# Sliding-window attention for two problems on one core: where the first V weights are issued, how many output staging buffers there are, and who casts and stores the last output tile

## The chip, the cores and the metric

The kernel runs on one core of a Trainium2 chip. The metric is the device time of one execution in microseconds (us), lower is better. All tensors in memory are bf16; the matrix products accumulate in f32.

## The reference, cut to what matters

Two independent problems, A and B, have the same shapes: `x` is 2048 rows of 1024, `wqkv` is 1024 x 3072 and `wo` is 1024 x 1024. Each is one attention layer with 32 heads of 32 columns and a causal window of 256 keys; the two results stand side by side in the output.

```python
qkv = (x @ wqkv).reshape(B, S, 3, H, Dh)              # S=2048, H=32, Dh=32
q, k, v = ...                                          # per head
scores = einsum("bhqd,bhkd->bhqk", q, k) * (Dh ** -0.5)
mask = (i - j >= 0) & (i - j < 256)
p = softmax(where(mask, scores, -1e9))
o = einsum("bhqk,bhkd->bhqd", p, v)
return o.reshape(B, S, D) @ wo
# result: concatenate([A, B], axis=-1), 2048 x 2048
```

## The kernel before, in words

The work is laid out for TensorE (PE), which is to be kept busy from start to end. `x` is held transposed, in tiles `xT` of 512 rows (four per problem, k = 0 to 3). Heads are taken in groups of four (128 columns); there are 8 groups per problem, 16 in all. A group needs its Q and K projections (`wqk` weights, lines 197 to 213) and its V projection (`wv` weights, two groups at a time, lines 215 to 236). Attention then runs in sessions of four key-by-query blocks: scores into PSUM (`st`, line 427), one exponential on ACT (line 435), two masks on POOL (lines 443 and 447), then products with V and with ones into `acc` (line 488), a reciprocal and a multiplication on DVE (lines 498 and 503) into `oT`.

The projections and the output products are cut into chains of eight matmuls. A planner with its own clock and cost table (`emit`, `level`, `forced`, `start_chain`) spreads these chains over the sessions. Each chain owns one of two PSUM banks (`pp`, pool `ps_proj`), and its result is moved out by `evacuate`, which picks ACT (line 189) or DVE (line 191) by the planner's clock. The order on each engine is the order in which the program is written; nothing reorders it afterwards.

**The start.** Rows of problem A's first 512 are loaded as they are (`xrow`, four transfers of 128 rows, in the buffer of an `oT` tile) on the SP queue, and PE transposes them (`flip`, line 549; ACT copies half of each result at line 553, DVE the other half at line 554, from the same PSUM bank). The other three tiles of A are transposed by DMA (`load_x`, line 132). The first weights, `wqk` for group 0 (two transfers of 256 KB) and `wv` for groups 0 and 1 (512 KB), are issued on ACT's queue, lines 520 to 522. A one-column POOL copy (line 524) reads `xrow[2]` and writes into the first `xT` tile that the DMA transposes: the transposing transfer, which writes the same tile, therefore waits on SP until the third set of rows has landed. Behind it on SP stand the two `wqk` transfers for group 1, the transposes of tiles 2 and 3 and the second `wv`.

**Loads later on.** Weights and B's `x` are loaded in pieces. `load_piece` writes one column with POOL (line 327) between two masks, and the piece's DMA on SP waits for that. SP is one queue in order: an output store that stands behind such a piece is issued after it.

**The output.** `out_steps` (lines 238 to 255) makes one 128 x 512 block of the output: eight matmuls, a cast into a staging tile `osb`, and a store on SP (line 252). `osb` comes from the pool `misc`, which has two buffers for each of its names. A cast into a buffer waits until the store that last read the buffer has landed. The casts of 21 of the 64 blocks start after 576 us, behind the last attention block. The last block is the last work of the kernel; after it each engine passes the branch at line 778, which skips a slower path for large inputs.

Of the kernel before, what the change touches and what calls it, by code (L numbers as in the profile page):

```python
# [8 lines left out]
BF16 = mybir.dt.bfloat16  # L9
# [9 lines left out]
P = 128  # L19
# [59 lines left out]
def _fast_path(ctx, tc, cfg, problems, outs, consts, certify):  # L79
    nc = tc.nc  # L80
    S, D, CT, T, NB = cfg.S, cfg.D, cfg.CT, cfg.T, cfg.NB
# [30 lines left out]
    ptp = ctx.enter_context(tc.tile_pool(name="pt", bufs=7))  # L112
    edgep = ctx.enter_context(tc.tile_pool(name="edge", bufs=2))
    misc = ctx.enter_context(tc.tile_pool(name="misc", bufs=2))
    once = ctx.enter_context(tc.tile_pool(name="once", bufs=1))
    ps_st = ctx.enter_context(tc.tile_pool(name="ps_st", bufs=1, space=PSUM))
    ps_acc = ctx.enter_context(tc.tile_pool(name="ps_acc", bufs=2, space=PSUM))
# [2 lines left out]
    xT, wqk, wv, wo_sb, vts, oTs, qks, pts = {}, {}, {}, {}, {}, {}, {}, {}  # L120
# [6 lines left out]
    def new_x(pi, k):  # L127
        xT[(pi, k)] = xpool.tile([P, CT, 512], BF16, name="xT")
# [7 lines left out]
    def wsrc(pi):  # L136
        return problems[pi][1].rearrange("(ct p) (k n) -> p ct k n", p=P, k=3)
# [4 lines left out]
    def load_wqk(g, which, queue, lo=0, hi=CT):  # L142
        pi, t = divmod(g, T)
        queue.dma_start(out=wqk[g][:, lo:hi, which, :],
                        in_=wsrc(pi)[:, lo:hi, which, t * P:(t + 1) * P])
# [4 lines left out]
    def load_wv(m, lo, hi, queue):  # L150
        pi, mm = divmod(m, T // VG)
        w_ = VG * P
        queue.dma_start(out=wv[m][:, lo:hi, :],
                        in_=wsrc(pi)[:, lo:hi, 2, mm * w_:(mm + 1) * w_])
# [14 lines left out]
    def by_columns(out, lo, hi, lhsT, rhs, start, stop):  # L169
        if whole[0]:  # L170
            nc.tensor.matmul(out[:, lo:hi], lhsT=lhsT, rhs=rhs, start=start, stop=stop,  # L171
                             skip_group_check=True)
            return
        for c in range(0, P, 32):
            nc.tensor.matmul(out[c:c + 32, lo:hi], lhsT=lhsT[:, c:c + 32], rhs=rhs, start=start,  # L175
                             stop=stop, tile_position=(0, c), skip_group_check=True)
# [10 lines left out]
    def evacuate(out, in_, engines=("act", "dve")):  # L187
        if clock.evacuate(engines) == "act":
            nc.scalar.copy(out=out, in_=in_)  # L189
        else:  # L190
            nc.vector.tensor_copy(out=out, in_=in_)

    def new_pp():
        clock.chain()
        return ps_proj.tile([P, 512], F32, name="pp")
# [42 lines left out]
    def out_steps(pi, b, ch):  # L238
        k, a = divmod(b, QB)
        st_ = {}  # L240
        steps = []
        for ct in range(CT):
            def f(ct=ct):
                if ct == 0:
                    st_["pp"] = new_pp()
                by_columns(st_["pp"], 0, 512, oTs[(pi, k)][:, ct, a * P:(a + 1) * P],
                           wo_sb[(pi, ch)][:, ct, :], ct == 0, ct == CT - 1)
                clock.pe += NS_MM
                if ct == CT - 1:
                    osb = misc.tile([P, 512], BF16, name="osb")  # L250
                    evacuate(osb[:], st_["pp"][:])
                    nc.sync.dma_start(out=outs[pi][b * P:(b + 1) * P, ch * 512:(ch + 1) * 512],
                                      in_=osb[:])
            steps.append((NS_MM, f))
        return steps

# [73 lines left out]
    chains = []  # L330
# [36 lines left out]
    current = []  # L367
# [149 lines left out]
    xrow = [rows[:, 2 * a:2 * a + 2, :].rearrange("p t n -> p (t n)") for a in range(QB)]  # L517
    for a in range(QB):
        nc.sync.dma_start(out=xrow[a], in_=problems[0][0][a * P:(a + 1) * P, :])
    for which in range(2):  # L520
        load_wqk(0, which, nc.scalar)
    load_wv(0, 0, CT, nc.scalar)
    new_x(0, 1)
    nc.gpsimd.tensor_copy(out=xT[(0, 1)][:, 0, 0:1], in_=xrow[2][:, 0:1])
    load_x(0, 1)
# [199 lines left out]
def kernel(  # L725
# [46 lines left out]
    with tc.manual_schedule():  # L772
        with ExitStack() as fctx:
            _fast_path(fctx, tc, cfg, problems, outs, consts, [reduce_bits, decide])
# [40 lines left out]
```

## Time and profile before

| | |
|---|---|
| median of 4 runs | 617.95 us (616.85 to 618.6) |
| the profiled execution | 618.5 us, span 616.7 us |
| PE busy | 594.5 us, 96% of the span |
| DVE busy | 505.5 us, 82% |
| ACT busy | 440.5 us, 71% |
| POOL busy | 320.2 us, 52% |
| mean granted TensorE clock | 0.995 of full |
| output stores (128 KB each, SP) | 64, median 1.7 us from issue to landing |

The span is what the profiler saw from the first to the last instruction of the core; 1.8 us of the execution's own time lie outside it. Busy times of PE are of overlapping, pipelined instructions. Lines of a timeline give the start, the duration, the engine, the source line, the operation and in brackets the idle time before it with what ended it. Lines of the chain of waits give start, duration and what the end of the kernel hung on at that time. Names ending in q (SPq, ACTq) are the queues of the engines' sequencers: a DMA's time there is that of its issue, not of its transfer.

### The profile page before, as it was taken

The numbers are of one execution on the slowest core, as the hardware profiler recorded it, in microseconds if no ns is written. First come the engines' busy times: TensorE is split into PE (matmuls) and PEld (weight loads), VectorE is DVE, ScalarE is ACT, GpSimd is POOL, SyncE is SP. The second block draws the span as 40 slices with busy tenths as digits, with TensorE's granted clock in tenths as the row PEclk, the third lists the DMA queues.
The fourth block names the chain that finished last, engine by engine and source line by source line (L and its number), as shares of the span: only waits on it lengthen the run. The fifth ranks groups of instructions, "written<-read, shape, count | busy, mean of one in ns | idle before, by whom it ended". The sixth has DMA issues, their size and how long they took to land.

```text
span 616.7 us, 27555 instructions
## 1 busy us (share of the span) xinstructions
PE 594.5 (96%) x12366; PEld 343.5 (56%) x12416; DVE 505.5 (82%) x816; ACT 440.5 (71%) x372; POOL 320.2 (52%) x631
## 2 busy tenths in 40 slices
PE   7999999999999999798999999999999999999996
PEld 5565466657555756454555665745445664444442
DVE  1588989999998999977999999887998999899200
ACT  3777878788878888666777777777877777775332
POOL 0565665655566566545555555555566555553000
PEclk9999999999999999989999999999999999999998
DMA  9923110111015501433001010112011030113222
GB/s 236 174 79 99 37 37 3 37 37 39 3 37 97 113 3 30 79 86 96 29 19 46 12 38 2 38 36 80 11 54 38 3 106 28 54 55 112 71 69 72
DMA packets 86652, 35.40 MB, mean 57 GB/s; under 512 B 65536, under 2 KB 86016, under 8 KB 86528
## 3 DMA queue, kind: packets, MB, share of 16 engines
q1 hardware_dynamic: 83408, 32.52, 21.3%
q8 instruction: 99, 1.62, 1.1%
q10 hardware_dynamic: 3120, 1.05, 0.7%
q14 instruction: 25, 0.20, 0.1%
HBM read 17.83 MB, written 8.39 MB: 43 GB/s over the span
## 4 chain that ended last, share of the span: by engine, by line
PE 86%; DMA 4%; DVE 2%; ACT 2%; issue 2%; POOL 1%; SPq 1%; ACTq 0%; DVEq 0%; POOLq 0%
PE pp L175 40%; PE pp L171 25%; PE acc L488 13%; PE st L427 9%; DMA out_dram<-osb 2%; DMA xT<-in_A_x_dram 1%; ACT pt L435 1%; DMA oT<-in_A_x_dram 1%; SPq L132 1%; DVE rinv L498 1%; POOL pt L443 1%; POOL pt L447 1%; DVE both L457 1%; ACT osb L189 0%; DVE top L183 0%
## 5 line engine op out<-in xcount | busy, mean ns | idle before, releaser
L435 ACT ACTIVATE pt<-st 128x2048 bf16<-128x2048 f32 x180 | 338.1, 1878 | 78.6 <-PE st L427 64.6
L498 DVE RECIPROCAL rinv<-acc 128x128 f32<-128x128 f32 x256 | 227.0, 924 | 31.2 <-PE acc L488 30.9
L447 POOL TENSOR_SCALAR_AFFINE_SELECT pt<-pt 128x512 bf16<-128x512 bf16 x224 | 150.8, 673 | 153.9 <-ACT pt L435 153.9
L443 POOL TENSOR_SCALAR_AFFINE_SELECT pt<-pt 128x512 bf16<-128x512 bf16 x256 | 176.4, 691 | 86.4 <-ACT pt L435 84.4
L175 PE MATMUL pp<-xT,wqk 128*32 128x512 bf16 x2688 | 160.7, 379 | 0.5 <-DMA xT<-in_B_x_dram 0.5
L457 DVE TENSOR_TENSOR both<-pt 128x512 bf16<-128x512 bf16 x224 | 130.3, 621 | 0.0
L175 PEld LDWEIGHTS <-wqk 128*32 128x32 bf16 x2688 | 71.4, 97 | 55.6 <-DMA xT<-in_B_x_dram 0.9
L171 PE MATMUL pp<-xT,wqk 128*128 128x512 bf16 (+1 forms) x331 | 80.2, 377 | 9.6 <-issue 3.3
L175 PE MATMUL pp<-wv,xT 128*32 128x256 bf16 x2548 | 78.6, 273 | 0.0
L427 PE MATMUL st<-qT,kT 32*128 32x384 bf16 (+2 forms) x1488 | 71.6, 269 | 0.8 <-ACT pt L435 0.7
L175 PEld LDWEIGHTS <-xT 128*32 128x32 bf16 x2548 | 68.3, 97 | 4.5
L171 PE MATMUL pp<-wo_sb,oT 128*128 128x512 bf16 x269 | 61.5, 379 | 2.4 <-issue 1.1
L488 PE MATMUL acc<-pt,vt 128*32 128x128 bf16 (+1 forms) x2160 | 63.4, 239 | 0.1
L189 ACT CAST osb<-pp 128x512 bf16<-128x512 f32 x52 | 30.3, 585 | 45.5 <-PE pp L171 23.1
L427 PEld LDWEIGHTS <-kT 32*128 32x128 bf16 x1488 | 22.5, 92 | 66.8 <-issue 66.3
L171 PEld LDWEIGHTS <-wqk 128*128 128x128 bf16 x368 | 34.1, 99 | 43.7 <-issue 13.8
L503 DVE TENSOR_TENSOR oT<-acc,rinv 128x256 bf16<-128x256 f32 x128 | 54.1, 423 | 3.7
L175 PE MATMUL pp<-wo_sb,oT 128*32 128x512 bf16 x920 | 54.0, 379 | 0.0
L488 PEld LDWEIGHTS <-vt 128*32 128x32 bf16 x2160 | 35.9, 96 | 26.5 <-issue 24.4
L171 PE MATMUL pp<-wv,xT 128*128 128x256 bf16 x387 | 47.3, 273 | 0.2 <-ACT kT L189 0.2
L171 PEld LDWEIGHTS <-oT 128*128 128x128 bf16 x282 | 26.8, 98 | 34.0 <-issue 3.2
L171 PEld LDWEIGHTS <-xT 128*128 128x128 bf16 x387 | 36.3, 98 | 10.4 <-issue 4.6
(43 smaller groups left out, 352.1 us busy)
## 6 DMA issues: line engine op xcount, KB each, us to landing
out_dram<-osb SPq DMA_DIRECT2D x64, 128.0 KB, 1.7
wqk<-in_B_wqkv_dram SPq DMA_DIRECT2D x32, 128.0 KB, 2.9
wqk<-in_A_wqkv_dram SPq DMA_DIRECT2D x24, 128.0 KB, 2.8
wo_sb<-in_A_wo_dram SPq DMA_DIRECT2D x16, 128.0 KB, 2.2
wv<-in_B_wqkv_dram SPq DMA_DIRECT2D x16, 128.0 KB, 2.4
wo_sb<-in_B_wo_dram SPq DMA_DIRECT2D x16, 128.0 KB, 2.3
oT<-in_A_x_dram SPq DMA_DIRECT2D x4, 256.0 KB, 5.2
wv<-in_A_wqkv_dram SPq DMA_DIRECT2D x8, 128.0 KB, 2.4
```

Source lines behind the costliest of these rows:

```text
L132: nc.sync.dma_start_transpose(out=xT[(pi, k)][:, c0:c1, lo:hi], in_=problems[pi][0][k * 512 + lo:k * 512 + hi, c0 * P:c1 * P])
L171: nc.tensor.matmul(out[:, lo:hi], lhsT=lhsT, rhs=rhs, start=start, stop=stop, skip_group_check=True)
L175: nc.tensor.matmul(out[c:c + 32, lo:hi], lhsT=lhsT[:, c:c + 32], rhs=rhs, start=start, stop=stop, tile_position=(0, c), skip_group_check=True)
L189: nc.scalar.copy(out=out, in_=in_)
L427: nc.tensor.matmul(st[:, r, a:b, :], lhsT=kT[32 * r:32 * r + 32, j * P:(j + 1) * P], rhs=qT[32 * r:32 * r + 32, q * P:(q + b - a) * P], st ...
L435: nc.scalar.activation(out=pt[:, :, :n, :].rearrange("p r a q -> p r (a q)"), in_=st[:, :, :n, :].rearrange("p r a q -> p r (a q)"), func= ...
L443: nc.gpsimd.affine_select(out=blk, in_=blk, pattern=[[0, 4], [1, P]], compare_op=ALU.is_ge, fill=0.0, base=0, channel_multiplier=-1)
L447: nc.gpsimd.affine_select(out=blk, in_=blk, pattern=[[0, 4], [-1, P]], compare_op=ALU.is_gt, fill=0.0, base=0, channel_multiplier=1)
L457: nc.vector.tensor_tensor(out=both[:, :, h, :], in0=pts[s0][:, :, a0, :], in1=pts[s1][:, :, a1, :], op=ALU.add)
L488: nc.tensor.matmul(acc[32 * r:32 * r + 32, which, o:o + w_], lhsT=lhsT, rhs=src[:, r, :, :], start=(x == 0), stop=(x == len(moves) - 1), t ...
L498: nc.vector.reciprocal(out=rinv[:, a * P:(a + 1) * P], in_=acc[:, 1, a * P:(a + 1) * P])
L503: nc.vector.tensor_tensor(out=oTs[(pi, k)][:, t, h * 256:(h + 1) * 256], in0=acc[:, 0, :], in1=rinv[:], op=ALU.mult)
```

## The change

Three edits. First, the 512 KB transfer of the first `wv` moves from ACT's queue to SP's, behind a second one-column POOL copy that reads `xrow[2]`; it now stands on SP between the row loads and the first DMA transpose. Second, `osb` gets a pool of its own with four buffers. Third, for the very last output block, ACT casts columns 0 to 287 and DVE columns 288 to 511, and the two parts are stored by ACT's queue and SP's queue; all other blocks go as before.

```diff
     misc = ctx.enter_context(tc.tile_pool(name="misc", bufs=2))
+    osbp = ctx.enter_context(tc.tile_pool(name="osb", bufs=4))
...
                 if ct == CT - 1:
-                    osb = misc.tile([P, 512], BF16, name="osb")
-                    evacuate(osb[:], st_["pp"][:])
-                    nc.sync.dma_start(out=outs[pi][b * P:(b + 1) * P, ch * 512:(ch + 1) * 512],
-                                      in_=osb[:])
+                    osb = osbp.tile([P, 512], BF16, name="osb")
+                    dst = outs[pi][b * P:(b + 1) * P, ch * 512:(ch + 1) * 512]
+                    if chains or current:
+                        evacuate(osb[:], st_["pp"][:])
+                        nc.sync.dma_start(out=dst, in_=osb[:])
+                    else:
+                        nc.scalar.copy(out=osb[:, 0:288], in_=st_["pp"][:, 0:288])
+                        nc.vector.tensor_copy(out=osb[:, 288:512], in_=st_["pp"][:, 288:512])
+                        nc.scalar.dma_start(out=dst[:, 0:288], in_=osb[:, 0:288])
+                        nc.sync.dma_start(out=dst[:, 288:512], in_=osb[:, 288:512])
...
     for which in range(2):
         load_wqk(0, which, nc.scalar)
-    load_wv(0, 0, CT, nc.scalar)
+    nc.gpsimd.tensor_copy(out=wv[0][:, 0, 0:1], in_=xrow[2][:, 0:1])
+    load_wv(0, 0, CT, nc.sync)
     new_x(0, 1)
     nc.gpsimd.tensor_copy(out=xT[(0, 1)][:, 0, 0:1], in_=xrow[2][:, 0:1])
     load_x(0, 1)
```

In the instructions as built, PE's are the same in kind and order. ACT loses one DMA issue at the start and has its last cast shorter with a DMA issue behind it; DVE gets one more cast at the end, POOL one more copy at the start, SP one more DMA at the start and a narrower one at the end. `evacuate` picks the same engine for every other block.

## The prediction

> **What bounds the kernel now.** I read the busy table first, then what PE waited for over the whole run, then the chain of waits around each of PE's gaps.
>
> ```profile
> PE 594.5 (96%) x12366; PEld 343.5 (56%) x12416; DVE 505.5 (82%) x816; ACT 440.5 (71%) x372; POOL 320.2 (52%) x631
> ```
>
> PE is busy for 594.5 of 616.7 us: only its 22 us of gaps can be won without less work. The waits of PE say whose they are (engine, line, what it waited for: us in total, times, longest).
>
> ```profile
> PE pp L171 <- ACT osb L189: 2.0, 3, 1.1
> PE pp L171 <- DMA xT<-in_A_x_dram: 0.8, 1, 0.8
> PE st L427 <- ACT pt L435: 0.7, 1, 0.7
> PE st L549 <- DMA oT<-in_A_x_dram: 0.5, 1, 0.5
> ```
>
> Three waits on an `osb` cast make 2.0 us. The largest wait, 3.2 us on POOL's `wv` pieces at 257.8 to 261.0, lies before the first `osb` and is not touched. Now the start, in the chain of waits:
>
> ```profile
> 1.73 5.73 DMA oT<-in_A_x_dram
> ...
> 7.51 0.20 POOL xT L524
> ...
> 7.72 4.06 SPq L132
> ...
> 11.84 0.57 SPq L144
> ...
> 12.45 0.58 SPq L144
> ...
> 13.07 8.90 DMA xT<-in_A_x_dram
> ...
> 22.01 2.10 PE pp L171 x9
> ```
>
> PE's first 22 us end on a chain without PE in it: the third rows land at 7.46, POOL's copy releases SP, SP issues the transpose of tile 1, two `wqk`, then the transpose of tile 2, which lands at 21.97. PE, idle for the last 0.78 us, goes on at 22.01. Whatever is won earlier by PE is lost again here.
>
> **Edit 1: wv to SP.** It takes a 2.00 us issue off ACT (1.93 to 3.93). That hides nothing of worth: ACT's table load then runs from about 1.95 to 3.2, but its first copy (5.25) needs PE's transposes, which end at 5.14. The edit adds a POOL copy (0.19 us) before the issue, and the second POOL copy runs while SP issues, so it costs nothing. On SP the issue of 512 KB lies ahead of the transpose of tile 1, both `wqk`, tiles 2 and 3 and the second `wv`. The same transfer on SP took 0.58 us to issue at 23.76; on ACT's filled queue 2.00. I take 0.6 with the gap.
>
> Its transfer moves too. DMA engines show a share of 0.95 or more from 2 us to 13 us, so 512 KB at the 277 to 330 GB/s of 7 to 9 us is 1.6 to 1.9 us of their time, now between release and first transpose. Tile 1 landed at 7.72 + 6.1 = 13.8 and is first read at 16.6: later by up to 1.9 it still is in time. `wv` itself was there at 10.1 (1.93 + 8.2). Issued at 7.7 with the 4.4 us of the second `wv` on SP it lands at 12.1; PE wants it at 12.7. Tile 3 landed at 25.8 (19.2 + 6.6) and `wqk` of group 1 is read only from 37.7; first read of tile 3 is at 28.3. Only tile 2 has no slack.
>
> How far tile 2 moves is bounded from both sides. Upper: the full 1.9 us. Lower: there is a hole in its transfer.
>
> ```profile
> 16.00:17.00 1.00, 1.00 (x10) 0.80 (x9) 0.06 (x1) 1.00 (x1) 0.00 (x0) 1.00 2.00 55
> 17.00:18.00 1.00, 0.95 (x11) 0.29 (x11) 0.64 (x1) 0.19 (x2) 0.81 (x2) 1.00 0.54 118
> ```
>
> The last column, GB/s, falls from 288 at 14 us to 55 and 118, while one 16 KB packet of the instruction queue is fetched in 15 to 18. Work that comes later may wait out the hole as tile 2 does now, so part or all of the shift vanishes. Also the rows may land sooner: at 2 to 4 us DMA moved 186 and 259 GB/s while ACT issued `wv`; at the 315 of 6 us those 445 KB take 1.4 instead of 2.0 us. More I don't grant, because the first 1.5 MB in line were rows and `wqk` and had passed only at about 7.2 us. So tile 2 moves by -0.6 to +1.9 us; I take +0.4, nearest to the 0.6 of SP's order less a part in the hole. PE's wait of 0.78 grows to about 1.2.
>
> **Edit 2: four buffers.** Each wait of PE in turn. At 283:
>
> ```profile
> 279.29 3.45 DMA out_dram<-osb
> ...
> 282.84 0.59 ACT osb L189
> ...
> 283.47 0.59 PE pp L171 x2
> ```
>
> The store before last, queued on SP behind pieces of `xT`, lands at 282.74; the cast waits for its buffer, PE 1.05 us for the bank. With a free buffer ACT casts at 280.0, when its exponential (278.14, 1.88 us) ends. PE goes on at 282.4. Next late is the scores' exponential: ready at 281.9, done at 283.8, wanted at 284.7 instead of 285.7. The 1.05 us stay won; PE shows no gap over 0.2 from there to 561. Waits of DVE (1.96 at 426.2) and ACT (1.10 at 463.1) on stores cost PE nothing. At 559 to 563:
>
> ```profile
> 558.81 0.58 ACT L189 CAST osb<-pp 128x512 bf16<-128x512 f32 x1 [2.10 <-DMA out_dram<-osb]
> ...
> 561.22 0.40 PE L427 MATMUL st<-qT,kT 32*128 32x128 bf16 x12 [0.72 <-ACT pt L435]
> ...
> 562.76 0.58 ACT L189 CAST osb<-pp 128x512 bf16<-128x512 f32 x1 [1.59 <-DMA out_dram<-osb]
> ...
> 563.40 1.89 PE L171 MATMUL pp<-wo_sb,oT 128*128 128x512 bf16 x8 [0.59 <-ACT osb L189]
> ```
>
> The late cast holds the exponential behind it on ACT, PE's scores 0.72; the next cast 0.59: 1.31 together. Next late is DVE, nearly without a gap from 555 to 572. PE's products at 569.45 need the bank that DVE's multiplication frees at 568.31 (567.90 + 0.41): 1.14 of the 1.31 are free, and DVE itself loses its 0.24 wait on a store. I take 1.2 (1.1 to 1.3). Last, 0.36 at 600.2 to 600.6, where a store took 4.1 instead of 1.7 us. Four buffers at one block per 1.73 us cover 4.1. Sum 1.05 + 1.2 + 0.36 = 2.6 us won (low 2.0, if the odd store is not there and half of 563 is lost; high 2.7).
>
> **Edit 3: the last block.** Two engines on one bank:
>
> ```profile
> 5.25 0.58 ACT L553 COPY xT<-acc 128x512 bf16<-128x512 bf16 x1
> ...
> 5.87 0.42 DVE L554 COPY xT<-acc 128x512 bf16<-128x512 bf16 x1 [4.61 <-ACT xT L553]
> ```
>
> Here too each engine took a half of one bank, and DVE began after ACT had ended. In the built order DVE's half again waits for ACT. So the casts add. ACT's 288 columns lie between 0.33 (288/512 of 0.585) and 0.585; with the slope from 512 columns (0.585) to 2048 (1.88), 0.40. DVE's 224 lie between 0.30 and 0.69; I take 0.40. In sequence 0.84 with the gap, against 0.585: SP's store is issued 0.25 later and is half as large. The last store took 2.8 us to land, the median one 1.7, so the luck of this one store swings up to 1.1 either way; ACT gets an issue of 0.3 to 0.6 ahead of its branch. I take +0.2 (-0.5 to +1.0).
>
> The Trainium skill speaks against this edit. "PSUM — Partial Sum Buffer", section "PSUM bank collisions raise a hardware error", has it that two engines must not read one bank and quadrant of partitions at once. By that rule the cost is the serial one above; by the wording of the change, two casts side by side, the last store would leave about 0.2 sooner. "DMA: Bandwidth & Descriptors", "Issuing engines are not separate DMA queues", adds that a second issuing engine saves issue time only.
>
> **Sum.** -2.6 + 0.4 + 0.2 = -2.0 us. The profiled execution (618.5, of which 616.7 span) becomes 616.5; it is 0.55 above the median of 617.95, which becomes 616.0. From no change a measurement of this kernel tells about 0.2%, 1.24 us.
>
> **The rivals.** (a) Slower: the weights block the queue. If `wv` on SP takes the 8.2 us of its ACT row, it lands at 15.9; PE waits 3.2 at 12.7, and tile 2 behind it lands 5.8 later (15.9 less 10.1). Then -2.6 + 5.8 + 0.2 = +3.4: 621.3. It beats the gain once tile 2 lands 2.4 us later than now. For it: SP is in order and the DMA engines are full. Against: those 8.2 us held 1 MB of rows and `wqk` ahead, which have nearly passed by 7.7; the second `wv` took 4.4. (b) No change: the whole 1.9 us reach tile 2, the tail costs 0.5: -2.6 + 1.9 + 0.5 = -0.2, 617.8. For it: the full DMA engines. Against: the hole. (c) The staging buffers don't do what they promise, because DVE and ACT take over as bound around 560: only 283 and a little more is won, -1.3 + 0.4 + 0.2 = -0.7, 617.3. Against: DVE's slack of 1.14. (d) Holding back does work: rows 0.6 sooner, shift swallowed, tail as lucky as the median store: -2.6 - 0.6 - 0.5 = -3.7, 614.3.
>
> **How the numbers follow.** The forecast gets 0.52; (a) 0.10, (b) 0.18, (c) 0.08, (d) 0.12. The main case spans 615.2 to 616.7 (-1.3 to -2.8). The range runs from 614.5, into (d), to 617.9, past (b), and leaves (a) out. Faster by over 0.2% (below 616.7) is the main case and (d): 0.64. (b) and (c) are the same: 0.26. Slower: (a), 0.10.
>
> **What would show it.** Right: PE's waits on `osb` at 283, 563 and 600 and the 0.72 on `pt` are gone, DVE's last cast begins after ACT's, PE's wait on `xT` at 22 us is about 1.2 instead of 0.78, and SP shows a `wv` issue at 7.7 of about 0.6 us. Wrong: a PE wait on `wv` near 12.8, a new PE wait on DVE near 568, tile 2 landing before 21.9 or after 24, or a tail from the last matmul to the end that differs from the present 5.6 us (611.1 to 616.7) by more than 1.

## The result, and the profile after

The changed kernel takes 616.52 us in the median (612.98 to 621.32), the kernel before 618.34 (615.35 to 623.82) in the runs beside it. The ratio is 0.9974, with a 95% interval of [0.9963, 0.9984]: 1.6 us less, between 1.0 and 2.3. The forecast was 2.0 less. The profiled execution took 614.69 us with a span of 613.0, so the two profiles lie 3.8 us apart, over twice what the medians say. That difference needs an explanation of its own.

The busy table shows the same work as before, in a shorter span:

```profile
PE 593.7 (97%) x12366; PEld 343.6 (56%) x12416; DVE 507.8 (83%) x817; ACT 440.6 (72%) x372; POOL 321.2 (52%) x632
```

The waits of PE (engine, line, what it waited for: us in total, times, longest). Lines have moved by one to eight: 171 is 172 now, 189 is 190, 427 is 434, 435 is 442, 549 is 557.

```profile
PE pp L172 <- POOL wv L334: 3.1, 1, 3.1
PE acc L557 <- DMA oT<-in_A_x_dram: 1.4, 2, 0.9
...
PE pp L172 <- DMA xT<-in_A_x_dram: 1.1, 1, 1.1
PE st L557 <- DMA oT<-in_A_x_dram: 0.6, 1, 0.6
PE pp L172 <- POOL xT L334: 0.3, 1, 0.3
```

No line names `osb` any more, and the 0.7 on `pt` is gone. The 0.5 on a piece of B's `xT` (line 175 before) is gone too, which no edit aimed at. The wait on A's `xT` is 1.1 instead of 0.8. The waits on the rows (`oT`) are not shorter: 1.4 and 0.6, where they were 1.3 and 0.5.

The start, in the chain of waits (start, duration, what the end hung on):

```profile
1.73 5.94 DMA oT<-in_A_x_dram
...
7.72 0.19 POOL wv L529
7.91 0.13 POOL xT L532
8.04 0.28 SPq L154
...
8.37 5.00 SPq L133
...
13.42 0.57 SPq L145
...
14.04 0.58 SPq L145
...
14.66 9.17 DMA xT<-in_A_x_dram
...
23.88 2.10 PE pp L172 x9
```

The third rows land at 7.67, not sooner than the 7.46 of before. Between them and the first transpose stand now two POOL copies and the issue of `wv` (8.04), and the issue of tile 1 itself takes 5.00 us where it took 4.06. Tile 2 lands at 23.83 instead of 21.97, which is 1.86 later. PE's wait on it grew by only 0.3, because PE itself came 1.56 later to the place; why is told under the hardware.

The hole in the transfers moved along with the work. The windows of a microsecond have the busy times of PE, PEld, DVE, ACT and POOL, then the granted clock, the DMA share and GB/s:

```profile
16.00:17.00 1.00, 1.00 (x16) 0.53 (x15) 0.00 (x0) 0.68 (x2) 0.00 (x0) 1.00 1.23 277
...
18.00:19.00 1.00, 0.95 (x7) 0.47 (x5) 0.49 (x1) 0.69 (x1) 0.24 (x1) 1.00 0.41 6
```

Before, 55 GB/s stood at 16 us; now 6 GB/s stand at 18. The 16 KB packet of the instruction queue, beside which the prediction saw the hole, starts at 17.7 instead of 15.6. The hole did not absorb the shift.

The places where PE waited for `osb`, in the timeline (start, duration, engine, line, operation, in brackets the idle time before and its releaser):

```profile
279.30 1.00 SPq L255 DMA_DIRECT2D out_dram<-osb  x2
...
280.21 0.58 ACT L190 CAST osb<-pp 128x512 bf16<-128x512 f32 x1
...
281.79 1.88 ACT L442 ACTIVATE pt<-st 128x2048 bf16<-128x2048 f32 x1 [1.01 <-PE st L434]
281.90 2.11 PE L172 MATMUL pp<-xT,wqk 128*128 128x512 bf16 x9 [0.16 <-issue]
```

```profile
558.45 0.59 ACT L190 CAST osb<-pp 128x512 bf16<-128x512 f32 x1 [0.40 <-ACT pt L442]
...
558.93 0.40 PE L434 MATMUL st<-qT,kT 32*128 32x128 bf16 x12
...
561.45 0.68 DVE L192 CAST osb<-pp 128x512 bf16<-128x512 f32 x1
...
562.96 3.64 PE L176 MATMUL pp<-wo_sb,oT 128*32 128x512 bf16 x64
```

The cast at 280.21 follows right behind ACT's work, at the 280 that the prediction named. At 558 to 563 neither the scores nor the products have an idle time in brackets, and PE waits for nothing of DVE's behind it.

The last block:

```profile
607.60 0.40 ACT L257 CAST osb<-pp 128x288 bf16<-128x288 f32 x1 [1.14 <-PE pp L172]
608.03 0.37 ACTq L259 DMA_DIRECT2D out_dram<-osb  x1
608.03 0.39 DVE L258 CAST osb<-pp 128x224 bf16<-128x224 f32 x1 [34.60 <-ACT osb L257]
608.45 0.33 SPq L260 DMA_DIRECT2D out_dram<-osb  x1
```

DVE's half waits for ACT's, 0.40 and 0.39 one after the other. PE's last matmul ends at 607.5, so the tail is 5.4 us instead of 5.6.

### The profile page after: what moved, and what is told of

Read it like the earlier page. It is cut to its first block, busy times and chain, and to the rows that moved or that the text cites. A ratio compares the mean times of both kernels' runs of the same rounds, so it can differ in the third digit from the quotient of the medians.

```text
span 613.0 us, 27536 instructions
## 1 busy us (share of the span) xinstructions
PE 593.7 (97%) x12366; PEld 343.6 (56%) x12416; DVE 507.8 (83%) x817; ACT 440.6 (72%) x372; POOL 321.2 (52%) x632
## 4 chain that ended last, share of the span: by engine, by line
PE 90%; DMA 2%; DVE 2%; issue 1%; SPq 1%; ACT 1%; POOL 0%; DVEq 0%; ACTq 0%
PE pp L176 42%; PE pp L172 26%; PE acc L495 13%; PE st L434 9%; DMA xT<-in_A_x_dram 1%; DMA oT<-in_A_x_dram 1%; ACT pt L442 1%; SPq L133 1%; DVE rinv L505 1%; DVE both L464 1%; DVE top L184 0%; POOL pt L454 0%; SPq L145 0%; SPq L526 0%; POOL pt L450 0%
## 5 line engine op out<-in xcount | busy, mean ns | idle before, releaser
L172 PEld LDWEIGHTS <-xT 128*128 128x128 bf16 x387 | 36.2, 98 | 10.5 <-issue 4.7
```

## The experiments

The theory was one of parts: the four buffers give all of the gain (staging), moving `wv` costs through its place on SP (order) or through its 512 KB ahead of the transposes (bytes, or data), and the split is worth little. The rival was the clock: PE's matmuls run at half rate for longer or shorter in one execution than in another, and what looks like a gain or a price of the edits is that.

**Four buffers only.**

```diff
+    osbp = ctx.enter_context(tc.tile_pool(name="osb", bufs=4))
...
-                    osb = misc.tile([P, 512], BF16, name="osb")
+                    osb = osbp.tile([P, 512], BF16, name="osb")
```

> Only the four staging buffers. By the forecast's sum this alone wins 2.6 us (ratio 0.9958), with PE's waits on osb casts gone and DVE the next to be late near 568. By the trace of the changed kernel, where the offset between the two kernels' matmuls falls by 1.2 at 283, 0.8 at 561, 0.8 at 563 and 0.5 at 600, it wins 3.3 us (0.9947). If the gain shown was made elsewhere, it wins under 1.5 us.

Measured: 615.86 us, ratio 0.9969 [0.9946, 0.9992], 1.9 us less (0.5 to 3.3). No wait of PE names `osb`. This part alone gives as much as the whole change, as far as the intervals tell; its own holds the 2.6 that was forecast and also values under 1.5, which would have spoken against it.

**`wv` behind the rows on SP only.**

```diff
-    load_wv(0, 0, CT, nc.scalar)
+    nc.gpsimd.tensor_copy(out=wv[0][:, 0, 0:1], in_=xrow[2][:, 0:1])
+    load_wv(0, 0, CT, nc.sync)
```

> Only the first V weights on SP behind the row loads. Theory A (order on SP): tile 2 of x lands later by the issue and the transfer ahead of it, PE's wait on it is over 0.78 us, and the kernel is slower by 0.4 to 1.9 us whatever PE's matmul rate does. Theory B (clock): the order costs next to nothing; what counts is when PE's matmuls go from twice to once their duration, 9.5 us in the kernel before, 12.5 us in the changed one. That time differs between executions with the same start, so the median differs from the kernel before by less than 0.6 us and the profile may show either time. If holding back helps the rows, the third rows land before 7.46 us and PE goes on at 22 us or sooner.

Measured: 619.62 us, ratio 1.0023 [0.9999, 1.0047], 1.4 us more (0 to 2.9). Its chain of waits shows the same two steps as the whole change, after rows that landed at 8.41:

```profile
8.77 0.28 SPq L153
...
9.10 5.02 SPq L132
...
15.41 8.87 DMA xT<-in_A_x_dram
```

The 1.4 is inside the 0.4 to 1.9 of the order theory and above the 0.6 of the clock theory, but the interval holds both. PE's wait on tile 2 is 1.6 in this profile, over the 0.78 that the order theory asked for, and the rows came later than 7.46, not sooner.

**The last block in halves only.**

```diff
+                    dst = outs[pi][b * P:(b + 1) * P, ch * 512:(ch + 1) * 512]
+                    if chains or current:
...
+                    else:
+                        nc.scalar.copy(out=osb[:, 0:288], in_=st_["pp"][:, 0:288])
+                        nc.vector.tensor_copy(out=osb[:, 288:512], in_=st_["pp"][:, 288:512])
+                        nc.scalar.dma_start(out=dst[:, 0:288], in_=osb[:, 0:288])
+                        nc.sync.dma_start(out=dst[:, 288:512], in_=osb[:, 288:512])
```

> Only the last block cast by ACT and DVE in two parts, stored by two queues. Forecast: +0.2 us (-0.5 to +1.0), inside what can be measured; DVE's part starts after ACT's ends; SP's last store is issued 0.25 us after the place it would have had. If the two casts ran side by side, the store would be issued about 0.2 us sooner than 0.61 us after the last cast began. The start of this kernel is that of the kernel before: by theory B its matmul rate may still double at another time than 9.5 us.

Measured: 618.2 us, ratio 1.0007 [0.9987, 1.0027]: no difference that can be told. From PE's last matmul to the end of the span, the three profiles with halves have 5.44, 5.45 and 5.49 us, the nine with one store 5.40 to 5.74, 5.61 in the mean. So the halves are worth about 0.15.

**Fillers, against the slow matmuls at the start.** Eight matmuls on zeros into an unused bank are put between the row transposes: one before the first, four before the second, three before the third. First with four buffers, `wv` on ACT as before:

```diff
+    def fill(n):
+        for _ in range(n):
+            nc.tensor.matmul(warm[:, 0:256], lhsT=blank[:, 0:P], rhs=blank[:, 0:256], start=True,
+                             stop=True)
+    fill(1)
     flip(0)
+    fill(4)
     flip(1)
+    fill(3)
     flip(2)
```

> Four staging buffers, wv left on ACT's queue, and filler matmuls (one, four and three of 256 columns) in PE's idle times before the transposes of the first three sets of rows. Theory B: PE is busy without a gap from 1.3 us on, its matmuls reach their short duration before 8.5 us, PE is at tile 2 up to 1.3 us sooner than in the kernel before, but then waits for tile 2, which lands at 22.0: only the time to 22 us is bounded by the DMA chain, so the gain over e1_osb4 is the cases in which the rate doubles late: 0 to 1 us. Theory A: no difference from e1_osb4 beyond 0.3 us.

Measured: 615.5 us, ratio 0.9953 [0.9934, 0.9971], 1.0 us below four buffers alone, with intervals that overlap. In the profile PE's matmuls are fast from 5.3 us on; PE comes to tile 2 1.56 us sooner than with four buffers alone and then waits 1.1 for it instead of 0.5. Then the fillers in the kernel before, with nothing else changed:

> The kernel before with eight filler matmuls between the row transposes at the start and nothing else changed. Staging theory (two buffers cost what the profiled executions show, 1.9 to 3.4 us): this run is 1.9 to 3.4 us above the run with four buffers and the same fillers, so its ratio is 0.998 to 1.001. Clock theory (a good part of the gain of four buffers with fillers came from the fillers): ratio 0.997 or lower. The profile should show PE waits on osb of 0.5 to 2 us in sum.

Measured: 618.22 us, ratio 0.9992 [0.9972, 1.0012], as the staging theory had it: the fillers give nothing by themselves that can be told, and between the two runs with fillers the four buffers are worth 0.39% or 2.4 us (0.7 to 4.1). Its timeline shows what two buffers cost in this execution:

```profile
562.20 0.40 PE L427 MATMUL st<-qT,kT 32*128 32x128 bf16 x12 [0.68 <-ACT pt L435]
...
564.30 1.89 PE L171 MATMUL pp<-wo_sb,oT 128*128 128x512 bf16 x8 [0.51 <-ACT osb L189]
```

These two are the ones of 561 and 563 in the profile before. The wait of 1.05 at 283 is not there: PE waited 1.7 us for a piece of B's `xT` just before, and none for a cast behind it.

And the fillers in the whole change:

> The whole change with the same fillers. Order theory (wv on SP moves the landing of tile 2 by 1.3 to 1.4 us against the landing of the third rows, 16.0 instead of 14.6, and PE meets it): 0.7 to 1.4 us above four buffers with fillers and wv on ACT, ratio about 0.997 if that one is again 0.995. Clock theory (the move of wv costs only through the slow matmuls at the start, which the fillers shorten): equal to it within 0.5 us, ratio about 0.9955.

Measured: 616.98 us, ratio 0.9978 [0.996, 0.9995], 1.5 us above four buffers with fillers (0.9953), though the two intervals just overlap. The profiles say the same without the times: behind tile 2 PE is 1.1 us later than with four buffers and fillers, and still is at 257 us. With PE early, the move of `wv` still costs; the clock theory of its price falls.

The fillers act at the start alone. Slow matmuls further on (last section) stand in five of the seven profiles with fillers. The mean granted clock of each execution is on record: 0.9952 in the mean over those of the change, and 0.9951 over the 87 of the kernel before that ran beside the experiments. So the clock does not make the 1.6 us of the change.

**The price of `wv`: order or bytes.** As four buffers with fillers, but `wv` held back by the POOL copy and issued on ACT:

```diff
-    load_wv(0, 0, CT, nc.scalar)
+    nc.gpsimd.tensor_copy(out=wv[0][:, 0, 0:1], in_=xrow[2][:, 0:1])
...
     fill(3)
+    load_wv(0, 0, CT, nc.scalar)
     flip(2)
```

> Four buffers and fillers, the first wv held back until the third rows have landed as in the change, but issued from ACT's queue (behind ACT's second row copy), so that nothing is added to SP. Order theory (SP's issue time is the price): the transpose of tile 1 takes about 4.1 us to issue again, tile 2 lands 14.4 to 14.9 us after the third rows, ratio as with wv unheld, 0.995. Data theory (the 512 KB that now stand behind the rows are the price): tile 1 takes 5.0 us to issue, tile 2 lands 15.6 to 16.2 us after the third rows, ratio 0.9965 to 0.9975. Holding back brings the rows forward: the third rows land at 7.0 or sooner instead of 7.5 to 8.0.

Measured: 617.49 us, ratio 0.9983 [0.9966, 0.9999]. The chain of waits:

```profile
7.89 5.49 SPq L133
...
14.67 8.39 DMA xT<-in_A_x_dram
```

Nothing of `wv` stands on SP now, and tile 1's issue takes even 5.49 us; tile 2 lands 15.6 us after the third rows. So the price does not need SP's order; it comes with the 512 KB behind the rows, whichever queue issues them. PE also waits 1.32 for `wv` itself at 12.1, which it does not in the change. And the rows landed at 7.50: holding 512 KB back brought them no nearer.

The starts of ten profiles side by side (us):

```
first wv        third rows land      issue of tile 1   tile 2 lands, after the third rows
early, on ACT   7.45 to 8.00 (six)   3.97 to 4.39      13.9 to 15.0, mean 14.5
held, on SP     7.61, 7.67, 8.41     4.88 to 5.02      15.1, 16.2, 15.9, mean 15.7
held, on ACT    7.50                 5.49              15.6
```

The means mix profiles with and without fillers; among those without, tile 2 moves by 1.2 (14.8 to 16.0), among those with fillers by 1.0 on SP and 1.4 on ACT.

The DMA engines show what holding back does. In the kernel before they move `wv` while the last rows land. With `wv` held they have next to nothing to move for about 1 us. The first line is the profile before, the second that of the change:

```profile
8.50:9.50 1.00, 1.00 (x7) 0.71 (x5) 0.31 (x1) 0.58 (x1) 0.00 (x0) 1.00 0.93 233
```

```profile
8.50:9.50 1.00, 1.00 (x8) 0.75 (x6) 0.09 (x1) 0.59 (x1) 0.00 (x0) 1.00 0.27 73
```

From 8 to 9 us it is 277 GB/s before and 1 after, and 0 with `wv` held on ACT. By 10 us 2.29 MB have moved before and 1.79 after: the difference is about the 512 KB of `wv`, which then take their time beside the transposes. That the idle time is the price fits all four profiles with `wv` held, which have 0 to 70 GB/s there, but no run separates it from the bytes.

**Tile 2 ahead of the weights.** If bytes in line are what counts, the two `wqk` transfers of group 1 can go behind:

```diff
+    new_x(0, 2)
+    load_x(0, 2)
     for which in range(2):
         load_wqk(1, which, nc.sync)
-    for k in range(2, NQ):
-        new_x(0, k)
-        load_x(0, k)
+    new_x(0, 3)
+    load_x(0, 3)
```

> Four buffers and fillers, wv unheld on ACT, and the transpose of tile 2 issued on SP ahead of the two wqk transfers of group 1. If the order on SP sets the landing of tile 2, it lands 1.2 us sooner or more (12.5 to 13.4 us after the third rows instead of 14.0 to 15.0) and PE's wait on it at 22 us, 0.8 to 1.1, is gone: 0.5 to 1.0 us below four buffers with fillers, ratio about 0.994. If DMA transposes land on a schedule of their own, nothing moves: 0.995.

Measured: 615.79 us, ratio 0.9961 [0.9946, 0.9977]; not below the 0.9953 without it. PE's wait on tile 2 is gone and stands one tile later, in the timeline:

```profile
28.09 1.47 PE L172 MATMUL pp<-xT,wqk 128*128 128x512 bf16 x6 [0.99 <-DMA xT<-in_A_x_dram]
```

The expected 0.5 to 1.0 was won at 22 us and lost at 28, to tile 3, which landed at 28.04, and at 25.41 with four buffers and fillers.

**Tiles 2 and 3 ahead.** The two `wqk` transfers go behind the loop over both tiles.

> Four buffers and fillers, wv unheld on ACT, and the transposes of both tile 2 and tile 3 issued on SP ahead of the two wqk transfers of group 1, which are read only from 37.7 us. Order theory: tile 2 lands by 20 us as in the run with tile 2 alone moved, tile 3 by about 26 instead of 28.0, so that the wait of 1.0 on it goes too: 1.0 to 1.9 us below four buffers with fillers, ratio 0.992 to 0.994. If a transpose of one tile cannot be brought below what it shows now whatever stands before it, or if the wait returns at wqk or the second wv: 0.995 to 0.996.

Measured: 614.56 us, ratio 0.9943 [0.9926, 0.996], the lowest of all, but just above the 0.992 to 0.994 that the order theory expected, and 0.6 us below four buffers with fillers where 1.0 to 1.9 were expected. The waits of PE have no line for A's `xT`:

```profile
PE pp L172 <- POOL wv L328: 2.4, 1, 2.4
PE pp L176 <- DMA xT<-in_B_x_dram: 1.6, 1, 1.6
PE pp L538 <- DVE top L125: 1.3, 1, 1.3
PE acc L550 <- DMA oT<-in_A_x_dram: 0.9, 1, 0.9
PE pp L172 <- ACT kT L190: 0.2, 1, 0.2
```

The waits are gone as foreseen. A gain over four buffers with fillers is not shown: the interval overlaps that of four buffers with fillers, and in this profile, with rows at 8.05 and slow matmuls until 10.5, PE is 0.3 us later at 257 us than in that one. This version beats the kernel before. By their ratios it also beats the change (0.9974 [0.9963, 0.9984]); but the kernel before had a mean granted clock of only 0.9941 in the executions beside this run, against 0.9959 in the run's own. Over all executions on record, an execution is about 0.45 us longer for each 0.001 of granted clock less (an estimate, by a straight line with a level for each kernel), so about 0.8 us of the lead can be the clock.

**Three buffers.** As four buffers with fillers, `bufs=3`.

> Three output staging buffers instead of four, with fillers, wv unheld on ACT. Staging theory: the casts at 559 and 562 wait for a store issued 2 blocks earlier; one more buffer already covers the 0.8 and most of the 0.75, so 1.2 to 1.5 us of the 1.9 that the two-buffer run with fillers loses are won, ratio 0.9955 to 0.9965, and PE shows no wait on osb over 0.2. If the fourth is needed: a wait on osb at 563 of 0.5 stays, ratio 0.997 or more.

Measured: 615.68 us, ratio 0.9949 [0.993, 0.9968], as with four (0.9953), a little below the 0.9955 to 0.9965 expected. PE waits for no `osb`. The fourth buffer is not needed.

## Why the prediction was right, point by point

How late the same PE instruction starts, against the profile before (us, the difference of its start in the two traces, at the time it has before):

```
                        21.9    257    270    281    284    560    561   564.5   601    end
the change             +1.86  +1.87  +0.29  -0.14  -1.35  -1.51  -2.30  -3.04  -3.57  -3.77
four buffers           +0.57  +0.77  +1.74  +2.66  +1.45  +1.30  +0.51  -0.23  -0.76  -0.73
wv on SP               +2.31  +2.48  +2.20  +2.39  +1.33  +1.48  +1.41  +1.40  +0.88  +0.63
halves                 +0.98  +0.99  -1.56  -0.35  -1.56  -1.45  -1.40  -1.48  -1.76  -1.96
fillers, two buffers   -0.06  -0.06  +0.88  +2.09  +0.88  +1.01  +0.98  +0.91  +0.51  +0.41
```

**Staging, -2.6 by the prediction.** The mechanism was right from 559 on and did not hold at 283. In the pair of profiles the change gains 3.4 from 281 to 601 (-0.14 to -3.57), and four buffers alone the same (+2.66 to -0.76). But the term was read from one execution. From 560 to 564.5 all kernels with four buffers gain 1.5, and those with two gain 0.1 at most: these 1.5 us are there every time (predicted 1.2). From 564.5 to 601 the other kernels with two buffers gain 0.3 to 0.5, where those with four gain 0.5, so most of the 0.36 at 600 is in one of four profiles with two buffers. So is the 283 wait (predicted 1.05). And it is the second of two waits at one place: about 2.5 us earlier PE waits for a piece of B's `xT`, in the profile before

```profile
PE pp L175 <- DMA xT<-in_B_x_dram: 0.5, 1, 0.5
```

and with four buffers alone

```profile
PE pp L176 <- DMA xT<-in_B_x_dram: 1.1, 1, 1.1
```

In the profile of the change this wait is absent; in the other six with three or four buffers it is 1.5 to 2.4. Over both waits, from 270 to 284, the change gains 1.64, four buffers alone 0.29, and `wv` on SP, with two buffers, 0.87. So the 1.05 at 283 is not shown to be won by the buffers. Counted from 281, between the two waits, two buffers cost 3.4, 1.9, 2.0 and 1.8 in the four profiles, on average 2.3, worked out as 3.4 less what each gains in these columns; counted from 284, behind both, 2.2, 1.8, 2.0 and 1.9, on average 2.0. The times say 1.9 (0.5 to 3.3) and 2.4 (0.7 to 4.1). So the 2.6 was 0.3 to 0.6 too high: 1.2 was too low, and 1.05 and 0.36 counted as steady what comes now and then.

**Start, +0.4 by the prediction, -0.6 to +1.9 as its bounds.** This step failed in size. Tile 2 moved by 1.86 in the profile and by 1.2 in the mean of the profiles (14.5 to 15.7 after the third rows), and the time by 1.4 (0 to 2.9). The prediction named the right terms, SP's order and the bytes, but let a hole in the transfers swallow most of them; the hole came later too. It did not see that the DMA engines would stand idle at 8 to 9 us. The order is 0.4 (from landing of the third rows to SP's first transpose 0.70 instead of 0.26), the slower issue of tile 1 is 0.8 (the means 4.17 and 4.97). That is the sum of 1.2 in the change; with `wv` held on ACT, where SP's order is as before, the issue of tile 1 alone is slower by 1.3.

**Tail, +0.2 (-0.5 to +1.0).** The casts came as sized, in sequence. The stores landed 2.65 and 2.46 us after their issue, the single one after 2.84. The last store took 2.6 to 2.9 in the eight of nine profiles with one store that show its landing, so the 2.8 that the prediction took for luck is what the last store takes here; why it isn't 1.7 stays open. The net is -0.15 by the profiles, not +0.2; the times can't tell either from nothing. The Trainium skill's page "PSUM — Partial Sum Buffer", section "PSUM bank collisions raise a hardware error", forbids two engines to read one bank and quadrant together; the built order puts DVE behind ACT, and all three profiles with halves show it, as 607.60 and 608.03 do here.

**The sum** with the measured terms is -2.3 + 1.2 - 0.15 = -1.25, or -0.95 with the -2.0 that is counted from 284, against -1.6 (-2.3 to -1.0) measured and -2.0 forecast. The forecast's errors, 0.3 to 0.6, 0.8 and 0.35, partly cancel, so it is in part luck that it came within 0.4. The times of the parts alone add up to -0.1 (-1.9, +1.4 and +0.4), but carry intervals of 1.2 to 1.5 us either way, so they cannot settle what is left. One more sentence of the prediction fails: that only the 22 us of PE's gaps can be won without less work. Slow matmuls count as busy, and 1.5 us of them stand at 262 (last section).

**Rivals.** (a) `wv` blocking the queue: it landed at 11.88, before PE wanted it, no wait; it fell. (b) The whole shift reaching tile 2: this is what happened at the start in the profile (1.86; 1.2 in the mean), but the no change that it foresaw did not follow: the tail cost nothing, and the mean shift is smaller. (c) DVE and ACT taking over at 560: no wait, all of 1.5 kept; it fell, and the 283 that it thought safe is what was not shown. (d) Rows sooner: 7.61 to 8.41 when held on SP, 7.50 when held on ACT, 7.45 to 8.00 when not held; it fell, and with it the only gain that the prediction had granted the move of `wv`.

**The signs.** Those for "right" came, but for the issue of `wv`, which took 0.38 us at 7.94 and not 0.6 at 7.7; none came for "wrong". One proved weak: PE's wait at 22 of about 1.2 came as 1.08 while the landing behind it moved by 1.86. The landing was the sign to ask for.

## What to carry to other kernels

Price a stall from several executions before calling it steady: of the waits on `osb` in one profile, those of 1.5 us came back in every profile with two buffers, the others did not, and one was only the second of two waits at the same place. Look at what the engine would wait for next if the stall went. Holding a transfer back can leave the DMA engines with nothing to do, and the bytes then stand beside the transfers on the path: here 512 KB held behind the rows cost 1.2 us at tile 2, whichever queue issued them. Look also at what in the line is read last, here the two `wqk`: with them behind tiles 2 and 3 the waits went, though a gain in time over four buffers with fillers is not shown. Three buffers did what four do.

## What the runs showed of the hardware

PE's clock differs from one execution to the next at the same place in the program. At the start, a 128x256 matmul takes 421 ns and later 273 (one starts every 213 ns, later every 109), with the change of pace at 9.4 us in the profile before and at 12.4 in the one after; elsewhere at 11.4 and 10.7, and with fillers at 4.8 to 7.5, but for one at 10.5. The granted clock shows 1.00 all through that stretch, so only the durations tell. In the profile of four buffers PE is slow until 4.8 us, then fast, slow and fast again. The lines show the fast stretch and the slow one behind it, with eight transposes in each of the first and last line and products with the weights between:

```profile
5.95 0.62 PE L550 MATMUL acc<-ident,oT 128*128 128x128 bf16 x8 [0.90 <-DMA oT<-in_A_x_dram]
...
8.07 1.70 PE L172 MATMUL pp<-xT,wqk 128*128 128x256 bf16 x8
9.56 1.06 PE L550 MATMUL acc<-ident,oT 128*128 128x128 bf16 x8
```

The slow stretch lasts from 8.3 to 11.7 us. At the start this costs nothing as long as PE then waits for tile 2 anyway: the column 21.9 above is the landing of tile 2 and nothing else, which is why fillers alone gave nothing.

In the middle it does cost. After the wait for POOL's `wv` pieces the same seven matmuls ran so in the profile before, and so after:

```profile
262.30 3.15 PE L171 MATMUL pp<-xT,wqk 128*128 128x512 bf16 x7 [0.24 <-POOL xT L327]
```

```profile
264.07 1.67 PE L172 MATMUL pp<-xT,wqk 128*128 128x512 bf16 x7 [0.27 <-POOL xT L334]
```

Here the granted clock agrees, 0.50 from 262 to 264 in the first and 1.00 in the second. That is 1.5 of the 3.8 us between the two profiles and is not tied to the change: 8 of the 12 profiles show slow matmuls there, for seven to all eleven of them, and the whole change with fillers is among the eight. Another 0.4 us is the wait for a piece of B's `xT` at 281, which the profile after does not have. The rest is the start (+1.86), the stretch from 281 to 601 (-3.4) and the tail (-0.2).

The Trainium skill's page "TensorE: Matmul & The Clock Gate", section "Part 1: The HAM clock gate (the "warmup" mystery)", has it that half rate is the default state of the clock, that a busy window of about 3.4 us lifts it and an idle one brings it back, and that the windows run freely, so that the point varies between runs. The stretch of 3.4 us in the profile of four buffers and the scatter of the start agree with it. The page's idle window of about 3.4 us is not what decides at 262: PE fell to half rate after a wait of 2.26 us (tile 2 ahead) and stayed at full rate after 3.07 (the change).
